# The last block of a fast-multiplication feed-forward kernel: another order of products, halves in the last product, other engines and queues for the outputs

## Chip, cores, metric

One core of one Trainium2 chip. The metric is the time of one execution on the device in microseconds (us), as the median of several executions. The profile's "span" is about 1.7 us shorter than this time (2424.1 beside 2425.77). "The kernel before" was timed again beside every other kernel on the same chip; the experiments ran on three chips, and its median there was 2425.88, 2425.92 and 2425.79.

## The reference

```python
# x: (8, 4096, 192) float32, weight: (8 heads, 7 taps)
w = softmax(weight, axis=-1)
y = causal_conv7(x, w)               # each head's 24 channels share 7 taps
y = y.reshape(32768, 192)
h = y @ w_in                         # (192, 2048)
g = h * (1.0 / (1.0 + np.exp(-h)))   # silu
out = g @ w_out                      # (2048, 192)
```

## The kernel before

The tokens are worked off in 32 blocks (`NB`) of 1024, each as two halves of 512 (`TB`). A block has an "up" phase (y @ w_in and silu) and a "down" phase (g @ w_out). Both replace eight products of quarter matrices by seven, at the price of sums and differences of operands and of results. In the down phase a block has four outputs, each 96 channels (`HD`) by 512 tokens: `c[0]` to `c[3]`. The products stand in six PSUM banks, `acc[0]` to `acc[5]`. The upper 96 rows of a bank hold one product, and its lower 32 rows a part of a product that is spread over three banks. Products with raw silu(h) need no work ahead of them; the others take differences `t(i)` that VectorE makes from `g`. "P1" is in `acc[0]`, "P3" in `acc[1]`; "C11" is `c[0]`.

The accumulators of the last weight group are finished in the order 0, 1, 2, 3, 5, 4; the last, bank 4, is one that uses differences:

```python
    def down(b, j):
        ...
        sets = ((1, 2, 0), (3, 2, 1), (6, 2, 2), (7, 4, 0), (5, 4, 1))
        every = slice(0, TB)
        for i in (0, 1, 2, 4, 3, 5) if j < NJ - 1 else (0, 1, 2, 3, 5, 4):
            if j == 0:
                accs[b][i] = bank()
            for e in range(2):
                if i < 5:
                    own, other, c = sets[i]
                    for q in range(NP):
                        lhs, rhs = forms[own]()
                        mm(i, q, every, lhs, q, rhs, e)
                    lhs, rhs = forms[other]()
                    mm(i, NP, every, lhs, c, rhs, e)
                # ... (i == 5: four matmuls of 128 columns)
                yield
```

The outputs are then sums of banks. A bank's rows are copied by ScalarE, and VectorE adds:

```python
    def merge(b, name):
        # ... ScalarE copies: x0..x2, y0..y2 (a bank's lower 32 rows), z1
        out_, u, v = {
            "M1": lambda: (c[1], c[0], acc[2][0:n, :]),
            "M2": lambda: (c[3], c[1], acc[1][0:n, :]),
            "M3": lambda: (c[2], c[1], acc[3][0:n, :]),
            "M4": lambda: (c[1], c[3], acc[4][0:n, :]),
            "M5": lambda: (c[3], c[2], acc[4][0:n, :]),
            "M6": lambda: (c[0], c[0], t["y"][0:n, :]),
            "M7": lambda: (c[2], c[2], t["x"][0:n, :]),
        }[name]()
        pin(nc.vector.tensor_tensor(out_, u, v, op=ALU.add))
```

VectorE transposes each output in tiles of 32 by 32, and it is stored in three pieces of 32 channels. Each piece is 64 KB. In the last block the pieces go over three queues:

```python
    def turn_out(b, i):
        ...
        pin(nc.vector.transpose(osb[...], cmbs[b][0][0:top, i, :]))
        for q in range(top // SQ):
            n, c = ...
            queue = (nc.sync, nc.scalar, nc.gpsimd)[q % 3] if b == NB - 1 else nc.sync
            queue.dma_start(
                out=out_v[2 * b + n][:, :, c : c + SQ], in_=osb[SQ * q : SQ * q + SQ, i, :, :]
            )
```

`pin` keeps an instruction at its place in its engine's program order.

Of the kernel before, what the change touches and what calls it, by code (L numbers as in the profile page):

```python
# [9 lines left out]
F32 = mybir.dt.float32  # L10
I32 = mybir.dt.int32
AF = mybir.ActivationFunctionType
ALU = mybir.AluOpType
# [4 lines left out]
def kernel(  # L18
# [24 lines left out]
    nc = tc.nc  # L43
# [6 lines left out]
    P = 128  # L50
# [4 lines left out]
    TB = 512  # L55
    TT = 2 * TB
    NB = NT // TT
    NCH = DFF // P
    NM = NCH // 2
    NJ = NM // 2  # L60
    SQ = 32
    HD = D // 2
    NP = HD // SQ
# [3 lines left out]
    out_v = out.rearrange("(n k t) d -> n t k d", k=TB // SQ, t=SQ)  # L67

    const = ctx.enter_context(tc.tile_pool(name="const", bufs=1))
    xpool = ctx.enter_context(tc.tile_pool(name="xp", bufs=1))  # L70
    tpool = ctx.enter_context(tc.tile_pool(name="tp", bufs=3))
    gpool = ctx.enter_context(tc.tile_pool(name="gp", bufs=2 * NJ))
    upool = ctx.enter_context(tc.tile_pool(name="up", bufs=13))
# [29 lines left out]
    def pin(ins):  # L103
        return tc.keep_in_program_order(ins)
# [8 lines left out]
    vec = Pinned(nc.vector)  # L113

    def bank():
        return psum.tile([P, TB], F32, tag="ps", name="ps")
# [3 lines left out]
    def load(b, ks=range(NK)):  # L120
# [14 lines left out]
        out=wexp.rearrange("p h k -> p (h k)"),  # L135
        in_=weight.rearrange("(o h) k -> o (h k)", o=1).to_broadcast([P, H * K]),
# [5 lines left out]
    for k in range(NK):  # L142
        nc.gpsimd.dma_start(
            out=xts[0][R:P, k, 0:pad], in_=x0[:, k, :], allow_slow_non_contiguous=True
# [142 lines left out]
    for e in range(2):  # L287
        half = hot[R * e : R * e + R]
        for sign, base in ((1, 0), (-1, grp - 1)):
            nc.gpsimd.affine_select(  # L290
                out=half,
                in_=half,
# [20 lines left out]
    for k in range(NK):  # L313
# [4 lines left out]
            op=ALU.mult,  # L318
# [96 lines left out]
    bk, us, sums, cmbs, accs = {}, {}, {}, {}, {}  # L415
# [63 lines left out]
        )[i]()  # L479
        pin(nc.vector.tensor_tensor(t[i // 2][:, i % 2, :], u, v, op=ALU.subtract))  # L480

    def down(b, j):



        if j == 0:
            accs[b] = {}
        g = [gs[b, j, a] for a in range(2)]
        w, x_ = wo[j], wx[j]

        def t(i):
            return sums[b, j][i // 2][:, i % 2, :].rearrange("p (e t) -> p e t", e=2)

        def mm(i, q, cols, lhs, c, rhs, e):
            pin(
                nc.tensor.matmul(  # L496
                    accs[b][i][SQ * q : SQ * q + SQ, cols],
                    lhs[:, e, SQ * c : SQ * c + SQ],
                    rhs[:, e, cols] if i < 5 else rhs[:, e, ts(q, TB // 4)],
                    start=j == 0 and e == 0,  # L500
                    stop=j == NJ - 1 and e == 1,
                    skip_group_check=True,
                )
            )

        a_ = [[w[:, a, :, HD * u : HD * u + HD] for a in range(2)] for u in range(2)]
        forms = {
            1: lambda: (a_[0][0], g[0][:, 0]),
            2: lambda: (a_[0][1], g[1][:, 0]),
            3: lambda: (x_[:, 2], g[1][:, 1]),  # L510
            4: lambda: (a_[1][1], t(3)),
            5: lambda: (x_[:, 0], t(0)),
            6: lambda: (x_[:, 1], t(1)),
            7: lambda: (a_[1][0], t(2)),
        }
        sets = ((1, 2, 0), (3, 2, 1), (6, 2, 2), (7, 4, 0), (5, 4, 1))
        every = slice(0, TB)

        for i in (0, 1, 2, 4, 3, 5) if j < NJ - 1 else (0, 1, 2, 3, 5, 4):
            if j == 0:  # L520
                accs[b][i] = bank()
            for e in range(2):
                if i < 5:
                    own, other, c = sets[i]
                    for q in range(NP):
                        lhs, rhs = forms[own]()
                        mm(i, q, every, lhs, q, rhs, e)
                    lhs, rhs = forms[other]()
                    mm(i, NP, every, lhs, c, rhs, e)
                else:  # L530
                    lhs, rhs = forms[4]()
                    for q in range(4):
                        mm(5, q, slice(0, TB // 4), lhs, 2, rhs, e)
                yield
        for a in range(2):
            del gs[b, j, a]
# [63 lines left out]
    osbs = {}  # L600

    def turn_out(b, i):
        if b not in osbs:
            osbs[b] = tpool.tile([P, 4, TB // SQ, SQ], F32, tag="t", name="osb")
        osb = osbs[b]
        top = HD if b else P
        pin(
            nc.vector.transpose(  # L608
                osb[0:top, i, :, :].rearrange("p k c -> p (k c)"), cmbs[b][0][0:top, i, :]
            )  # L610
        )
        for q in range(top // SQ):
            n, c = (i % 2, HD * (i // 2) + SQ * q) if b else (q // 2, R * i + SQ * (q % 2))
            queue = (nc.sync, nc.scalar, nc.gpsimd)[q % 3] if b == NB - 1 else nc.sync
            queue.dma_start(  # L615
                out=out_v[2 * b + n][:, :, c : c + SQ], in_=osb[SQ * q : SQ * q + SQ, i, :, :]
            )

    plan = [slot.split() for slot in PLAN.split("|")]
    NU = NM * 11 // 2  # L620
    did = set()

    def step(b, token):

        if token[0] == "-":
            b, token = b - 1, token[1:]
        name, arg = token.split(".") if "." in token else ("", "")
        if b < 0 or b >= NB or not name or (b, token) in did:
            return
        did.add((b, token))  # L630
        digits = [int(c) for c in arg]
        if name[0] in "PE":
            product(b, digits[0], name)
        elif name[0] in "sCg":
            if b:
                sums_h(b, name, digits[0])
        elif name == "t":
            sum_g(b, *digits)
        elif name[0] in "Mzyx":
            merge(b, name)  # L640
        elif name == "o":
            turn_out(b, *digits)
        elif b + 1 < NB:
            {"i": turn_in, "v": conv, "w": win}[name](b + 1, *digits)
            if name == "v" and digits[1] == K - 1 and (b, "down") in did:
                spread(b + 1, digits[0])
                if digits[0] == NK - 1 and b + 2 < NB:
                    load(b + 2)

    def begin_down(b):  # L650
        did.add((b, "down"))
        for k in range(NK):
            if b + 1 < NB and (b, f"v.{k}{K - 1}") in did:
                spread(b + 1, k)

    def run(b, slots):
        for s in slots:
            for token in s:
                step(b, token)


    for k in range(NK):
# [31 lines left out]
    for k in range(NK):  # L694
        turn_out(0, k)
# [3 lines left out]
    for b in range(1, NB):  # L699
        run(b, plan[: NU // 4])  # L700
        if b == 1:
            for j in range(NJ):
                combine_out(j)
        run(b, plan[NU // 4 : NU])
        begin_down(b)
        slots = (None for j in range(NJ) for _ in down(b, j))
        for s in plan[NU:]:
            next(slots)
            run(b, [s])
        assert next(slots, 0) == 0  # L710
    run(NB, plan[:NU])


# [28 lines left out]
```

## Time and profile before

All times below are on the trace's own clock, from the start of the span. The prediction shows the profile lines they come from. TensorE works without a break to 2412.22, so the first 99.5% of the span are not in question here; the tail behind it is.

| kernel before | us |
|---|---|
| median time | 2425.77 |
| span | 2424.1 |
| TensorE's end | 2412.22 |
| VectorE's last transpose ends | 2417.24 |
| last store issued (start): GpSimd's; SyncE and ScalarE 2417.27 | 2417.64 |
| last store landed | 2422.24 |
| end | 2424.07 |

The tail is read as a relay: TensorE's end, the last data in its final form, the last store's issue, its landing, the end.

### The profile page before, as it was taken

How to read it: one execution, taken by the hardware profiler on the slowest of the kernel's cores; microseconds unless marked ns; L12 is line 12 of the kernel's file. 1: busy time of each engine (PE TensorE's matmuls, PEld its weight loads, DVE VectorE, ACT ScalarE, POOL GpSimd, SP SyncE). 2: the span in 40 equal slices, each digit the busy share in tenths (PEclk: the TensorE clock that was granted, in tenths of full speed). 3: DMA queues.
4: the chain of work that ended last, by engine and by line, in shares of the span. 5: the costliest groups of instructions: out<-in, count | busy, mean ns of one | idle time of the engine just before them, and what ended most of it. 6: DMA issues, size and time to landing. Idle time of an engine off the chain costs nothing.

```text
span 2424.1 us, 43022 instructions
## 1 busy us (share of the span) xinstructions
PE 2389.0 (99%) x17744; PEld 944.2 (39%) x17744; DVE 2076.5 (86%) x2827; ACT 981.7 (40%) x1845; POOL 66.4 (3%) x100
## 2 busy tenths in 40 slices
PE   6999999999999999999999999999999999999998
PEld 3344433334433334333444333443334443334432
DVE  8988888898888888888988889888889888898875
ACT  3134533345433345333454333553334543335432
POOL 3300000000000000000000000000000000000000
PEclk9999999999999999999999999999999999999999
DMA  7321222222222212221222222122222222221220
GB/s 151 73 52 32 44 44 53 41 43 40 36 53 50 43 32 42 47 53 40 41 41 39 53 48 46 31 39 50 53 40 40 38 43 53 46 43 36 36 40 14
DMA packets 452005, 111.65 MB, mean 46 GB/s; under 512 B 421792, under 2 KB 426912, under 8 KB 451808
## 3 DMA queue, kind: packets, MB, share of 16 engines
q1 hardware_dynamic: 447888, 106.63, 23.6%
q8 instruction: 139, 2.28, 0.4%
q0 software_dynamic: 608, 1.84, 0.4%
q10 hardware_dynamic: 3312, 0.42, 0.1%
q14 instruction: 58, 0.48, 0.1%
HBM read 31.49 MB, written 25.17 MB: 23 GB/s over the span
## 4 chain that ended last, share of the span: by engine, by line
PE 98%; DVE 1%; DMA 0%; SPq 0%; ACT 0%; issue 0%; POOL 0%; ACTq 0%; POOLq 0%; DVEq 0%
PE ps L439 49%; PE ps L496 46%; PE ps L547 2%; PE ps L403 1%; DVE nat L353 0%; DVE two L111 0%; SPq L127 0%; DMA nat<-in_x_dram 0%; DVE cmb L598 0%; DMA raw<-in_moe_w_in_dram 0%; DVE mh L111 0%; DVE wr L111 0%; DVE xt L333 0%; POOL out_dram L615 0%; DVE osb L608 0%
## 5 line engine op out<-in xcount | busy, mean ns | idle before, releaser
L439 PE MATMUL ps<-dup,ws 64*128 64x512 f32 x2480 | 869.1, 589 | 0.0
L496 PE MATMUL ps<-g,wo 128*32 128x512 f32 x2976 | 662.0, 593 | 0.0
L463 DVE TENSOR_TENSOR g<-u,ps 128x512 f32<-128x512 f32 x744 | 485.6, 680 | 117.6 <-PE ps L439 88.8
L439 PE MATMUL ps<-win,wr 64*128 64x512 f32 x1488 | 568.8, 589 | 0.1
L496 PE MATMUL ps<-t,wo 128*32 128x512 f32 (+1 forms) x4464 | 500.7, 450 | 0.0
L460 ACT ACTIVATE g<-g 128x512 f32<-128x512 f32 x744 | 444.7, 631 | 99.9 <-DVE g L463 99.9
L439 PEld LDWEIGHTS ps<-dup,ws 64*128 64x128 f32 x2480 | 363.8, 187 | 289.5 <-issue 273.8
L496 PE MATMUL ps<-t,wx 128*32 128x512 f32 x2976 | 453.0, 592 | 0.0
L353 DVE SCALAR_TENSOR_TENSOR nat<-xt,taps,nat 128x512 f32<-128x512 f32 x576 | 432.0, 750 | 15.1
L439 PE MATMUL ps<-dup,wr 64*128 64x512 f32 x992 | 419.3, 596 | 0.0
L454 ACT COPY u<-ps 128x512 f32<-128x512 f32 x496 | 277.5, 588 | 228.7 <-PE ps L439 225.8
L586 ACT COPY cmb<-ps 96x512 f32<-96x512 f32 x31 | 18.0, 581 | 832.2 <-PE ps L496 832.2
L480 DVE TENSOR_TENSOR t<-g 128x1024 f32<-128x1024 f32 x248 | 299.8, 1220 | 26.7 <-PE ps L496 26.7
L480 DVE TENSOR_TENSOR t<-g,t 128x1024 f32<-128x1024 f32 x248 | 303.4, 1224 | 18.3 <-PE ps L496 7.4
L439 PEld LDWEIGHTS ps<-win,wr 64*128 64x128 f32 x1488 | 234.0, 187 | 174.6 <-issue 145.7
L496 PEld LDWEIGHTS ps<-t,wo 128*32 128x32 f32 x4464 | 178.3, 110 | 222.6 <-issue 205.2
L439 PE MATMUL ps<-win,ws 64*128 64x512 f32 x496 | 241.5, 589 | 0.0
L496 PE MATMUL ps<-g,wx 128*32 128x512 f32 x1488 | 234.7, 592 | 0.0
L496 PEld LDWEIGHTS ps<-t,wx 128*32 128x32 f32 x2976 | 121.9, 110 | 278.2 <-issue 268.7
L598 DVE TENSOR_TENSOR cmb<-cmb,ps 96x512 f32<-96x512 f32 x155 | 105.7, 682 | 141.9 <-ACT u L583 139.7
L439 PEld LDWEIGHTS ps<-dup,wr 64*128 64x128 f32 x992 | 160.8, 187 | 127.2 <-issue 112.0
L496 PEld LDWEIGHTS ps<-g,wo 128*32 128x32 f32 x2976 | 168.5, 110 | 97.7 <-issue 97.7
(56 smaller groups left out, 1194.6 us busy)
## 6 DMA issues: line engine op xcount, KB each, us to landing
dup<-nat SPq DMA_DIRECT2D x384, 128.0 KB, 2.3
nat<-in_x_dram SPq DMA_DIRECT2D x382, 64.0 KB, 2.4
out_dram<-osb SPq DMA_DIRECT2D x376, 64.0 KB, 2.0
raw<-in_moe_w_in_dram SPq DMA_DIRECT2D x16, 192.0 KB, 4.8
raw<-in_moe_w_out_dram SPq DMA_DIRECT2D x8, 384.0 KB, 3.6
ws<-wr POOLq DMA_DIRECT2D x8, 192.0 KB, 4.4
xt<-xt SPq DMA_DIRECT2D x31, 4.5 KB, 1.9
tail<-xt SPq DMA_DIRECT2D x24, 4.5 KB, 1.9
```

The source lines that it names most:

```text
L353: nc.vector.scalar_tensor_tensor(out=dst, in0=src, scalar=tap, in1=dst, op0=ALU.mult, op1=ALU.add)
L403: nc.tensor.matmul(hs[a, n, e], rows(wr[j], e)[:, a, k, :], rows(d, e)[:, n, k, :], start=k == 0, stop=k == NK - 1,)
L439: nc.tensor.matmul(bk[b, m, bn], rows(w, half), rows(v, half), start=first, stop=True, skip_group_check=True,)
L454: pin(copy(u, bk[b, m, "1"]))
L460: pin(nc.scalar.activation(g, g, AF.Silu))
L463: pin(nc.vector.tensor_tensor(g, us.pop((b, m, i)), bk[b, m, bn], op=ALU.add))
L480: pin(nc.vector.tensor_tensor(t[i // 2][:, i % 2, :], u, v, op=ALU.subtract))
L496: nc.tensor.matmul(accs[b][i][SQ * q : SQ * q + SQ, cols], lhs[:, e, SQ * c : SQ * c + SQ], rhs[:, e, cols] if i < 5 else rhs[:, e, ts(q, ...
L547: nc.tensor.matmul(acc[k][R * n : R * n + R, :], wo[j][:, a, e, R * k : R * k + R], gs[b, j, a][:, n, e, :], start=j == 0 and a == 0 and e ...
L586: pin(nc.scalar.copy(c[0], acc[0][0:n, :]))
L598: pin(nc.vector.tensor_tensor(out_, u, v, op=ALU.add))
```

## The change

The intent: let the products that need no differences come last in the last block; let four outputs be nearly complete by then, so that the last sums are short; let two outputs leave while TensorE still works; split the last product's columns into halves so that the first half is worked on while the second is computed. GpSimd takes the sum of C11. The stores use two queues (SyncE, ScalarE, SyncE) and no longer GpSimd's.

```diff
-    def down(b, j):
+    def out_slot(b, j, i, e, half=None):
+        ...   # the four matmuls of accumulator i, optionally for one half of the columns
...
-            queue = (nc.sync, nc.scalar, nc.gpsimd)[q % 3] if b == NB - 1 else nc.sync
-            queue.dma_start(
+            nc.sync.dma_start(
...
+    def finish(b):
+        late = (NJ - 2, NJ - 1)
+        for j in late:
+            ...                                   # differences
+            for i in (2, 4, 3, 5):
+                for e in range(2):
+                    out_slot(b, j, i, e)
+        ...
+        def store(i, cols, rows_=slice(0, n)):
+            ...
+            vec.transpose(osb[rows_, cols], cmb[rows_, i, cols])
+            for q in range(rows_.start // SQ, rows_.stop // SQ):
+                (nc.sync, nc.scalar, nc.sync)[q % 3].dma_start(...)
+        ...                                       # sums over accumulators 2 to 5
+        for j in late:
+            for e in range(2):
+                out_slot(b, j, 0, e)
+        for half in range(2):
+            for j in late:
+                for e in range(2):
+                    out_slot(b, j, 1, e, half)
+            if half == 0:
+                for k in (3, 2):
+                    add(c[k], c[k], acc[0][0:n, :])
+                    store(k, every)
+                add(c[1], c[1], acc[0][0:n, :])
+                pin(nc.scalar.copy(c[0], acc[0][0:n, :]))
+                pin(nc.scalar.copy(part(y, 0), acc[0][n:P, :]))
+        for half in range(2):
+            cols = slice(half * TB // 2, (half + 1) * TB // 2)
+            add(c[1][:, cols], c[1][:, cols], acc[1][0:n, cols])
+            pin(nc.scalar.copy(part(y, 1)[:, cols], acc[1][n:P, cols]))
+            store(1, cols)
+            nc.gpsimd.tensor_tensor(c[0][:, cols], c[0][:, cols], y[0:n, cols], op=ALU.add)
+            store(0, cols)
...
-    run(NB, plan[:NU])
+    finish(NB - 1)
```

More of the change, by code (lines that the diff above doesn't have):

```diff
@@ L480, in sum_g, with t @@
         pin(nc.vector.tensor_tensor(t[i // 2][:, i % 2, :], u, v, op=ALU.subtract))
-    def down(b, j):
-        if j == 0:
-            accs[b] = {}
+    def out_slot(b, j, i, e, half=None):
         g = [gs[b, j, a] for a in range(2)]
         w, x_ = wo[j], wx[j]
-        def t(i):
-            return sums[b, j][i // 2][:, i % 2, :].rearrange("p (e t) -> p e t", e=2)
-        def mm(i, q, cols, lhs, c, rhs, e):
-            pin(
-                nc.tensor.matmul(
-                    accs[b][i][SQ * q : SQ * q + SQ, cols],
-                    lhs[:, e, SQ * c : SQ * c + SQ],
-                    rhs[:, e, cols] if i < 5 else rhs[:, e, ts(q, TB // 4)],
-                    start=j == 0 and e == 0,
-                    stop=j == NJ - 1 and e == 1,
-                    skip_group_check=True,
-                )
-            )
+        if i not in accs.setdefault(b, {}):
+            accs[b][i] = bank()
+        def t(k):
+            return sums[b, j][k // 2][:, k % 2, :].rearrange("p (e t) -> p e t", e=2)
         a_ = [[w[:, a, :, HD * u : HD * u + HD] for a in range(2)] for u in range(2)]
@@ L515, in down @@
         }
-        sets = ((1, 2, 0), (3, 2, 1), (6, 2, 2), (7, 4, 0), (5, 4, 1))
-        every = slice(0, TB)
+        own, other, c = ((1, 2, 0), (3, 2, 1), (6, 2, 2), (7, 4, 0), (5, 4, 1), (4, 4, 2))[i]
+        for q in range(4):
+            lhs, rhs = forms[own if q < NP else other]()
+            k = c if i == 5 or q == NP else q
+            to = slice(0, TB // 4) if i == 5 else slice(0, TB) if half is None else ts(half, TB // 2)
+            pin(
+                nc.tensor.matmul(
+                    accs[b][i][SQ * q : SQ * q + SQ, to],
+                    lhs[:, e, SQ * k : SQ * k + SQ],
+                    rhs[:, e, ts(q, TB // 4) if i == 5 else to],
+                    start=j == 0 and e == 0,
+                    stop=j == NJ - 1 and e == 1,
+                    skip_group_check=True,
+                )
+            )
+    def down(b, j):
         for i in (0, 1, 2, 4, 3, 5) if j < NJ - 1 else (0, 1, 2, 3, 5, 4):
-            if j == 0:
-                accs[b][i] = bank()
             for e in range(2):
-                if i < 5:
-                    own, other, c = sets[i]
-                    for q in range(NP):
-                        lhs, rhs = forms[own]()
-                        mm(i, q, every, lhs, q, rhs, e)
-                    lhs, rhs = forms[other]()
-                    mm(i, NP, every, lhs, c, rhs, e)
-                else:
-                    lhs, rhs = forms[4]()
-                    for q in range(4):
-                        mm(5, q, slice(0, TB // 4), lhs, 2, rhs, e)
+                out_slot(b, j, i, e)
                 yield
@@ L659, in run, with part, add @@
                 step(b, token)
+    def finish(b):
+        late = (NJ - 2, NJ - 1)
+        for j in late:
+            for k in (0, 1, 3, 2):
+                step(b, f"t.{j}{k}")
+            for i in (2, 4, 3, 5):
+                for e in range(2):
+                    out_slot(b, j, i, e)
+        acc, n = accs[b], HD
+        cmb = xpool.tile([P, 4, TB], F32, tag="cmb", name="cmb")
+        cmbs[b] = [cmb]
+        c = [cmb[0:n, i, :] for i in range(4)]
+        y, x_ = (upool.tile([P, TB], F32, tag="u", name="u") for _ in range(2))
+        def part(t, k):
+            return t[SQ * k : SQ * k + SQ, :]
+        def add(out_, u, v):
+            vec.tensor_tensor(out_, u, v, op=ALU.add)
+        def store(i, cols, rows_=slice(0, n)):
+            if b not in osbs:
+                osbs[b] = tpool.tile([P, 4, TB // SQ, SQ], F32, tag="t", name="osb")
+            osb = osbs[b][:, i, :, :].rearrange("p k c -> p (k c)")
+            vec.transpose(osb[rows_, cols], cmb[rows_, i, cols])
+            ks = slice(cols.start // SQ, cols.stop // SQ)
+            for q in range(rows_.start // SQ, rows_.stop // SQ):
+                ch = HD * (i // 2) + SQ * q
+                (nc.sync, nc.scalar, nc.sync)[q % 3].dma_start(
+                    out=out_v[2 * b + i % 2][:, ks, ch : ch + SQ],
+                    in_=osbs[b][SQ * q : SQ * q + SQ, i, ks, :],
+                )
+        every = slice(0, TB)
+        pin(nc.scalar.copy(c[1], acc[2][0:n, :]))
+        pin(nc.scalar.copy(part(y, 2), acc[2][n:P, :]))
+        pin(nc.scalar.copy(part(x_, 1), acc[4][n:P, :]))
+        add(c[2], c[1], acc[3][0:n, :])
+        pin(nc.scalar.copy(part(x_, 0), acc[3][n:P, :]))
+        add(c[3], c[2], acc[4][0:n, :])
+        add(c[1], c[1], acc[4][0:n, :])
+        for q in range(4):
+            pin(
+                nc.scalar.copy(
+                    part(x_, 2)[:, ts(q, TB // 4)], acc[5][SQ * q : SQ * q + SQ, 0 : TB // 4]
+                )
+            )
+        add(c[2], c[2], x_[0:n, :])
+        for j in late:
[19 more added lines that the diff above has]
+            store(0, cols)
@@ L705 @@
         begin_down(b)
-        slots = (None for j in range(NJ) for _ in down(b, j))
-        for s in plan[NU:]:
-            next(slots)
+        last = b == NB - 1
+        if last:
+            did.update((b, t.lstrip("-")) for s in plan for t in s if t.lstrip("-")[0] in "Mzyxo")
+        slots = (None for j in range(NJ // 2 if last else NJ) for _ in down(b, j))
+        for s, _ in zip(plan[NU:], slots):
             run(b, [s])
         assert next(slots, 0) == 0
-    run(NB, plan[:NU])
+    finish(NB - 1)
 _INS = ['x', 'weight', 'moe_w_in', 'moe_w_out']
```

## The prediction

> **What bounds the kernel now.** I read the page first: the span, TensorE's busy share and the chain of work that ended last.
>
> ```profile
> span 2424.1 us, 43022 instructions
> PE 2389.0 (99%) x17744; PEld 944.2 (39%) x17744; DVE 2076.5 (86%) x2827; ACT 981.7 (40%) x1845; POOL 66.4 (3%) x100
> PE 98%; DVE 1%; DMA 0%; SPq 0%; ACT 0%; issue 0%; POOL 0%; ACTq 0%; POOLq 0%; DVEq 0%
> ```
>
> TensorE carries 98% of the chain. The change touches only the second half of the last of 32 blocks and keeps TensorE's column count, so it can win only where TensorE no longer works. The busy time by stretch says how much that is (columns: PE, weight loads, DVE, ACT, POOL; then clock, DMA share, GB/s):
>
> ```profile
> 2403.00:2412.30 9.30, 9.22 (x104) 2.92 (x96) 3.65 (x6) 3.92 (x9) 0.00 (x0) 1.00 0.01 2
> 2412.30:2424.10 11.80, 0.00 (x0) 0.00 (x0) 3.86 (x6) 0.58 (x1) 2.61 (x4) 0.64 0.40 67
> ```
>
> TensorE ends at 2412.22; the remaining 11.85 us (0.5% of the span) are the tail, and all that is at stake. The chain in order of time shows its first half:
>
> ```profile
> 2412.28 0.38 ACTq L615
> ...
> 2412.70 0.59 ACT u L583
> ...
> 2413.31 0.70 DVE cmb L598
> ...
> 2414.03 0.69 DVE cmb L598
> ...
> 2414.75 0.69 DVE cmb L598
> 2415.43 0.63 DVE osb L608
> 2416.07 0.28 issue
> 2416.35 1.29 POOL out_dram L615 x2
> 2417.64 0.64 POOLq L737
> ```
>
> ScalarE first issues a store (0.38), then copies the last bank's lower rows (0.59); VectorE makes three dependent sums (about 0.72 each) and three transposes (0.6 apart), so the last stores start at 2417.27. Then only stores and the closing remain. SyncE's waits and the landing times of the stores issued after 2417.2 show the second half:
>
> ```profile
> SPq L737 <- DMA out_dram<-osb: 4.5, 1, 4.5
> ```
> ```profile
> out_dram<-osb POOLq DMA_DIRECT2D x2, 64.0 KB, 4.3
> out_dram<-osb SPq DMA_DIRECT2D x1, 64.0 KB, 4.6
> out_dram<-osb ACTq DMA_DIRECT2D x1, 64.0 KB, 4.8
> ```
>
> They take 4.3 to 4.8 us, because nine of the twelve stores of 64 KB are issued within 1.6 us (2416.08 to 2417.64). The three issued near 2412.3 had the engines to themselves:
>
> ```profile
> out_dram<-osb SPq DMA_DIRECT2D x1, 64.0 KB, 2.1
> out_dram<-osb ACTq DMA_DIRECT2D x1, 64.0 KB, 2.4
> out_dram<-osb POOLq DMA_DIRECT2D x1, 64.0 KB, 2.7
> ```
>
> The last landing is at 2422.25, the end at 2424.07: closing takes 1.8 us. The tail is thus 5.05 (sums to last issue) + 5.0 (backlog of stores) + 1.8.
>
> **What the Trainium skill says.** (1) "PSUM — Partial Sum Buffer", section "PSUM bank collisions raise a hardware error": two engines must not touch one bank and 32-partition quadrant at once, even in different columns; guard by bank. The built program agrees: in the changed kernel VectorE's first half-sum from P3's bank waits for TensorE's count 8888, the last matmul of the second half. No run yet shows it in time. (2) "DMA: Bandwidth & Descriptors", "Issuing engines are not separate DMA queues": stores from several queues share the same DMA engines, and only issue time is saved. The trace agrees: three queues, and still 4.3 to 4.8 us under backlog against 2.1 to 2.7. (3) "GPSIMD Engine Reference", "Elementwise — side-by-side cycle accounting": about 2.6 cycles an element for a two-input float32 add (at its 1.2 GHz 2.2 ns). The trace has it on an idle chip, at 584 ns for 192 elements and 456 for 128, so 2.0 ns an element:
>
> ```profile
> L254 POOL TENSOR_TENSOR wo<-wo 128x192 f32<-128x192 f32 x4 | 2.2, 584 | 0.0
> L254 POOL TENSOR_TENSOR wr<-wr 128x128 f32<-128x128 f32 x3 | 1.3, 456 | 0.1
> ```
>
> **The change, part by part.** *TensorE.* The last two weight groups first give accumulators 2, 4, 3 and 5, which use differences, then accumulator 0, then accumulator 1 (P3) in two halves of 256 columns. A quad of 512-column matmuls takes 0.43 us, one of 128 columns 0.107, so it is linear and 256 columns cost 0.215. The order of sums on VectorE (due 2392 to 2400) stays ahead of their use. From 2393.99: differences done at 2405.1, accumulator 0 at 2408.6, first half of P3 at 2410.3, all at 2412.0 plus 0.2 of drain. TensorE's end stays at 2412.2: gain 0.
>
> *Hidden under TensorE.* The four sums over accumulators 2 to 5 run from 2405.0 to 2408.1. Accumulator 0 is readable at 2408.8; then VectorE does sum, transpose, sum, transpose, sum (pitches of 0.6 to 0.72), to 2412.17. So six of the twelve stores are issued at 2410.3 to 2412.0 and land by about 2414.5. Before, only three were out by then. Backlog mostly gone.
>
> *On the path after TensorE.* Durations of halves are estimates from the rows: VectorE 0.684 us for 512 columns less 256/0.96 ns = 0.42; transpose 0.40; ScalarE 0.579 and 0.255 for 512 and 128 give 0.36; GpSimd 0.456 + 128 x 2.0 ns = 0.71, plus 0.08 to start.
> - VectorE's half sum 2412.31 to 2412.74. But since VectorE reads accumulator 0 first, ScalarE's two copies of that bank (0.58 each) start only after VectorE's third sum, at 2412.22, and end at 2413.39; P3's half copy follows, to 2413.77.
> - GpSimd half 0: 2413.85 to 2414.56. VectorE's transpose of it to 2415.0, and only then, in program order, the second half sum, 2414.95 to 2415.37.
> - ScalarE has meanwhile two stores ahead of its second copy; it copies 2415.45 to 2415.81; GpSimd half 1 2415.9 to 2416.6; last transpose to 2417.05.
>
> So the last data is ready at 2417.05, just 0.2 us earlier than before: two serial half chains (2.7 and 2.1 us) take the place of one chain of full size.
>
> *Stores.* The three after that are 32 KB each. SyncE carries two of each three. Every store waits for the previous one on its semaphore of eight: SyncE's second-half store of c1 waits for a ScalarE store issued at 2415.04 (lands near 2417.0), the first of the last pair for one issued at 2415.83 (lands near 2417.8). I take 2417.85 and 2418.2 for the last two issues, 0.35 later than data alone would allow for each. A half-size store without backlog: 2.1 less some 0.3 = 1.8 us, landing at 2420.0. The saving against 2422.25 is 2.25 us.
>
> *Closing.* Before, the first of nine waits in a row was the last store's (a GpSimd one), and the eight others followed at 0.06 each. Now the last to land is among the final three: 0.4 less, so 1.4. End 2421.4 against 2424.07: 2.65 less. I give 0.1 back for unmodelled queue steps: 2425.77 - 2.57 = 2423.2.
>
> **The rivals.** *Halves overlap as intended*: if the first half's sum started when its matmuls end (2410.5), the first half chain would hide and the end fall 2 us more, to about 2421.2. For it speaks the code's order; against it the wait for count 8888. *GpSimd slow*: beside VectorE's work the trace shows 0.77 us for 128 elements instead of 0.456; if that held at 256, each half costs about 0.5 more, and two of them 1 us: 2424.2. Against it: VectorE waits at that moment. *Stores still bound*: if landings stay near 3 to 4 us or the semaphore chain on SyncE slips by one landing more, 2424.3 to 2425. *TensorE stalls* on differences or on 256-column weight loads (0.13 us per quad of loads, under 0.215 of matmul): 0.3 to 1 us back; the stretches show no idle time, so unlikely.
>
> **Range and chances.** The gain can hardly pass the tail less one bare chain (sum, copy, add, transpose, store, closing: about 6.5 us). Each term above is uncertain by some 0.3, GpSimd and the store waits by 0.5 to 1, mostly on the slow side: 2422.3 to 2424.3. 2% is 48.5 us, four times the whole tail, so within 2% is nearly certain: faster 0.003, within 0.995, slower 0.002.
>
> **What would show each step.** TensorE's end within 0.2 us of 2412.2, without idle time. No VectorE sum from P3's bank before it. ScalarE's two copies of accumulator 0 right after VectorE's third sum of it, ahead of P3's first half copy. GpSimd adds near 0.7 us each, 2 us apart. Last store issued near 2418.2, landing within 2 us; waits of SyncE for landed stores between its own. A half sum starting near 2410.5, GpSimd adds over 1 us, or last landings of 3 us and more would show the prediction wrong, as would a tail shorter than 8 us or longer than 10.5.

## The result, and the profile after

The kernel after took 2423.11 us in the median of six runs (2422.77 to 2423.26), beside 2425.83 for the kernel before in six (2425.73 to 2426.24): 2.72 us less. The ratio is 0.9988 (interval 0.9975 to 1.0001). Ratios here and below are the mean time of one kernel's fast runs over the mean of the other's fast runs of the same rounds, so not quite the ratio of the quoted medians. The interval reaches 1, but the two sets of runs lie 2.5 us apart at their nearest, and each set is only 0.5 us wide; I take the 2.7 us as real for that reason. The traced run is the fastest of the six: its span is 2421.0, those of the others 2421.2 to 2421.5.

First the page of the kernel after, with span and busy times:

```profile
span 2421.0 us, 43109 instructions
PE 2389.7 (99%) x17776; PEld 953.3 (39%) x17776; DVE 2077.5 (86%) x2831; ACT 983.3 (41%) x1847; POOL 65.3 (3%) x98
```

TensorE's busy time has not fallen; it has 32 more, shorter matmuls. Then the busy time by stretch of the kernel after (same columns as in the prediction):

```profile
2403.00:2412.30 9.30, 9.16 (x132) 3.89 (x124) 5.96 (x10) 2.30 (x7) 0.00 (x0) 1.00 0.11 17
2412.30:2421.00 8.70, 0.00 (x0) 0.00 (x0) 2.42 (x6) 1.78 (x4) 1.44 (x2) 0.75 0.49 75
```

TensorE's last matmul still ends at 2412.2, and the stretch behind it has shrunk from 11.8 to 8.7 us. VectorE now works 5.96 us of the last stretch under TensorE, against 3.65 before, and the DMA share there is 0.11 against 0.01: that is what was moved forward. The chain of the kernel after, in order of time, is the leg from accumulator 0 to the last data:

```profile
2411.52 0.58 DVE cmb L111
...
2412.18 0.53 ACT cmb L714
...
2412.77 0.58 ACT u L715
...
2413.53 0.23 ACT u L719
...
2413.82 0.72 POOL cmb L721
2414.54 1.33 issue
2415.87 0.77 POOLq L802
...
2416.66 0.44 DVE osb L111
```

VectorE's third sum from P1's bank ends at 2412.10; only then ScalarE copies that bank (in two copies), then P3's first half, and GpSimd adds. The row "issue 1.33" hides a second round through all engines: VectorE transposes the first half's result, makes the second half's sum (2414.95), ScalarE copies (2415.47), GpSimd adds again (2415.91 to 2416.63). The last data is final at 2417.10, as late as before.

SyncE's waits on landed stores at the store line (L682), and the landing times of the stores issued from 2417 on:

```profile
SPq L682 <- DMA out_dram<-osb: 1.5, 3, 0.7
```
```profile
out_dram<-osb SPq DMA_DIRECT2D x3, 32.0 KB, 1.6
out_dram<-osb ACTq DMA_DIRECT2D x1, 32.0 KB, 1.6
```

SyncE waits three times, 0.7 us at most, for an earlier store to land before it can issue the next. The last of these waits ends at 2417.40, when a ScalarE store has landed; the next-to-last store is issued at 2417.48, the last one at 2418.15, a microsecond after the data. But a store, now of half the size, lands in 1.6 us (median; the last one took 1.86), where the kernel before needed 4.3 to 4.8.

| leg, us | before | predicted | after |
|---|---|---|---|
| TensorE's end | 2412.22 | 2412.2 | 2412.16 |
| last data final | 2417.24 | 2417.05 | 2417.10 |
| last issue | 2417.64 | 2418.2 | 2418.15 |
| last landing | 2422.24 | 2420.0 | 2420.00 |
| end | 2424.07 | 2421.4 | 2421.04 |

By legs: the last issue is 0.51 later, the landing after it 2.75 shorter (4.61 to 1.86), the closing 0.79 shorter (1.83 to 1.04). Sum: 3.03 less in the traces, and 2.7 in the medians.

So the reorganised arithmetic gave almost nothing on the data's own leg (0.1); the time came out of the stores and the closing. Which part of the change did that is the question of the experiments.

### The profile page after: what moved, and what is told of

It is laid out like the page before. It is cut to its first block, busy times and chain, and to the rows that moved or that the text cites. A ratio compares the mean times of both kernels' runs of the same rounds, so it can differ in the third digit from the quotient of the medians.

```text
span 2421.0 us, 43109 instructions
## 1 busy us (share of the span) xinstructions
PE 2389.7 (99%) x17776; PEld 953.3 (39%) x17776; DVE 2077.5 (86%) x2831; ACT 983.3 (41%) x1847; POOL 65.3 (3%) x98
## 4 chain that ended last, share of the span: by engine, by line
PE 98%; DVE 1%; DMA 0%; SPq 0%; issue 0%; ACT 0%; POOLq 0%; POOL 0%; ACTq 0%; DVEq 0%
PE ps L439 49%; PE ps L510 46%; PE ps L538 2%; PE ps L403 2%; DVE nat L353 0%; SPq L127 0%; DMA nat<-in_x_dram 0%; DMA raw<-in_moe_w_in_dram 0%; DVE two L111 0%; DVE cmb L111 0%; DVE osb L111 0%; DVE xt L333 0%; DVE nat L350 0%; ACT two L201 0%; DVE mh L111 0%
## 5 line engine op out<-in xcount | busy, mean ns | idle before, releaser
L510 PE MATMUL ps<-g,wx 128*32 128x512 f32 (+1 forms) x1512 | 234.6, 585 | 0.0
```

The source lines that it names most:

```text
L510: nc.tensor.matmul(accs[b][i][SQ * q : SQ * q + SQ, to], lhs[:, e, SQ * k : SQ * k + SQ], rhs[:, e, ts(q, TB // 4) if i == 5 else to], sta ...
```

## The experiments

Theory A (the prediction's): the halves on TensorE do nothing, because VectorE may read P3's bank only after its last matmul; the serial half chains cost what they save; the gain is that six stores leave early. The rivals are named with each run. Twelve kernels ran, all with correct results.

The traces start up unevenly. In the kernel after and in experiment 3, which are the same program up to the last sums, the same matmul starts at 170.95 and at 171.28 us, and TensorE ends at 2412.16 and 2412.49; over all kernels its end lies between 2412.06 and 2412.50. Where a leg is compared between two traces below, it is therefore counted from TensorE's end. In the kernel after the last data is final 4.94 us behind it, the last store issued at 5.98, landed at 7.84, and the end comes at 8.88; in the kernel before the four are 5.03, 5.42, 10.03 and 11.86.

**1. P3 in one piece on TensorE** (halves stay in the sums and stores).

```diff
-        for half in range(2):
+        for half in range(1):
             for j in late:
                 for e in range(2):
-                    out_slot(b, j, 1, e, half)
+                    out_slot(b, j, 1, e)
```

> P3 in one piece of 512 columns on TensorE; the sums, copies and stores after it still by halves. Theory A (the gain is the stores of two outputs that leave under TensorE; TensorE's halves do nothing, as the first half sum waits for the last matmul anyway): the first half sum starts at the same 2412.2, the time stays within 0.2 us of the changed kernel's 2423.1. Rival B (halves overlap TensorE with the sums): the half sum starts later and the time rises by 1 us or more.

Measured: 2422.90 (2422.63 to 2423.54), ratio 0.9988. The first half sum started at 2412.13 against 2412.23, 0.07 us behind TensorE's end in both. Halves on TensorE are worth nothing here, as Theory A has it.

**2. No halves at all**: experiment 1, and sums, copies and stores of whole outputs.

```diff
-        for half in range(2):
-            cols = ...
-            add(c[1][:, cols], ...); copy(part(y, 1)[:, cols], ...); store(1, cols)
-            nc.gpsimd.tensor_tensor(c[0][:, cols], c[0][:, cols], y[0:n, cols], op=ALU.add)
-            store(0, cols)
+        add(c[1], c[1], acc[1][0:n, :])
+        pin(nc.scalar.copy(part(y, 1), acc[1][n:P, :]))
+        store(1, every)
+        nc.gpsimd.tensor_tensor(c[0], c[0], y[0:n, :], op=ALU.add)
+        store(0, every)
```

> No halves anywhere: P3 whole, one sum of 512 columns, one copy, one GpSimd add, whole stores. Theory A: one chain takes the place of two serial half chains: sum to 2412.95, ScalarE's P1 copies to 2413.36, copy to 2413.95, GpSimd 1.23 us to 2415.25, transpose to 2415.95, last store near 2416.35, landing after 2.3, closing 1.05: end near 2419.8, so 1.2 us below the changed kernel (about 2421.9). Rival B: slower than the changed kernel by 0.5 us or more, because nothing is pipelined any more.

Measured: 2421.81 (2421.62 to 2422.13), ratio 0.9983. GpSimd's timeline in this kernel (start, duration, engine and form; in brackets the idle time ahead and what ended it) and the last row of its chain, VectorE's last transpose, show why:

```profile
2414.06 1.26 POOL L719 TENSOR_TENSOR cmb<-cmb,u 96x512 f32<-96x512 f32 x1 [168.81 <-ACT u L717]
```
```profile
2415.35 0.71 DVE osb L111
```

One GpSimd sum of 1.26 us replaces two of 0.72 with a whole round between them, so the last data is final at 2416.06 instead of 2417.10, and there are 12 stores instead of 18 (8 instead of 12 on SyncE), the last issued at 2416.45. The halves of sums and stores thus *cost* 1.1 us, against experiment 1, which differs in nothing else (1.3 against the kernel after): the split was made for an overlap that doesn't occur.

**3. P1's three sums first**, then ScalarE's copies of that bank, then the transposes.

```diff
-                for k in (3, 2):
-                    add(c[k], c[k], acc[0][0:n, :])
-                    store(k, every)
-                add(c[1], c[1], acc[0][0:n, :])
+                for k in (3, 2, 1):
+                    add(c[k], c[k], acc[0][0:n, :])
                 pin(nc.scalar.copy(c[0], acc[0][0:n, :]))
                 pin(nc.scalar.copy(part(y, 0), acc[0][n:P, :]))
+                for k in (3, 2):
+                    store(k, every)
```

> Halves kept; VectorE makes its three sums from P1's bank one after the other, then the transposes, so that ScalarE can copy P1's bank from 2410.7 on instead of 2412.2. Theory A: P3's first half copy then starts at 2412.7 instead of 2413.4, everything after it 0.7 us earlier: about 2422.4. Rival (ScalarE's copies are not on the path; the end hangs on stores alone): within 0.2 us of 2423.1, or slower, as the two hidden outputs leave later.

Measured: 2422.99 (2422.90 to 2423.07), a miss. Counted from TensorE's end, the last data was final 0.75 us earlier (4.19 instead of 4.94), as expected, but SyncE issued its last store at 5.93 instead of 5.98, and it landed at 7.81 instead of 7.84. SyncE waited four times for a landed store, 1.0 us in all (three times and 1.5 in the kernel after). With these 18 stores, data that comes earlier meets a queue that isn't free: the rival, that the end hangs on the stores, is right here.

**4. VectorE sums C11** in place of GpSimd.

```diff
-            nc.gpsimd.tensor_tensor(c[0][:, cols], c[0][:, cols], y[0:n, cols], op=ALU.add)
+            add(c[0][:, cols], c[0][:, cols], y[0:n, cols])
```

> C11 summed on VectorE instead of GpSimd, the rest as changed. Theory A: 0.42 us in place of 0.72 plus 0.08 to start, twice on the path: 0.7 us earlier, about 2422.4. Rival C (GpSimd relieves a busy VectorE): slower by 0.3 us or more, because VectorE has three more kinds of work there.

Measured: 2422.66 (2422.58 to 2422.98). The half sum took 0.42 us on VectorE against 0.72 on GpSimd and the last data was final 0.7 earlier (2416.39), but the last issue was only 0.4 earlier (2417.73), and the last landing 0.15 (2419.85), as that store took 2.12 us instead of 1.86. GpSimd costs 0.7 on the data's leg; the stores pass on less of it, 0.45 by the medians and 0.14 by the two traces.

**5. Sums first, halves only up to the transpose, whole stores.** Experiment 3, with the stores of outputs 1 and 0 sent whole after the second half.

```diff
             store(1, cols)              # now: transpose only
+            if half:
+                send(1, every)
             nc.gpsimd.tensor_tensor(c[0][:, cols], c[0][:, cols], y[0:n, cols], op=ALU.add)
             store(0, cols)              # now: transpose only
+        send(0, every)
```

> As the run with VectorE's three sums first (halves kept in sums, copies and transposes), but all four outputs leave in whole stores, 12 instead of 18. After that run the theory is: in the changed kernel the end hangs on SyncE's queue of stores, whose last three wait for landings of earlier ones, so earlier data gained 0.1 us only. Then with whole stores the earlier data counts: last data near 2416.4, last issue 2416.8, landing 2419.1, closing 1.05: time near 2421.9, 1.1 below. Rival (it is the number of bytes in flight, or the sums themselves): no better than 2422.7.

Measured: 2422.22 (2422.08 to 2422.54). Against experiment 3 the stores alone changed, and it is 0.77 faster: counted from TensorE's end, the last issue came at 4.61 instead of 5.93, although a whole store has to wait for both halves; the landing (2.75 instead of 1.88) gave 0.9 of that 1.3 back. It is 0.3 slower than I expected.

**6. Whole pieces, sums first, VectorE for C11**: the three findings together (2, 3 and 4).

```diff
+                for k in (3, 2, 1):
+                    add(c[k], c[k], acc[0][0:n, :])
                 ...   # ScalarE's copies of acc[0]
+                for k in (3, 2):
+                    store(k, every)
+        add(c[1], c[1], acc[1][0:n, :])
+        pin(nc.scalar.copy(part(y, 1), acc[1][n:P, :]))
+        store(1, every)
+        add(c[0], c[0], y[0:n, :])
+        store(0, every)
```

> No halves, VectorE's three sums of P1's bank first, C11 summed on VectorE. If the terms of the path add up: P3's sum to 2412.95, copy to 2413.53, VectorE's sum of C11 to 2414.25, transpose to 2415.0, last issue 2415.45, landing 2.4, closing 1.1: end 2419.0, time near 2420.7, 1.1 below the run without halves. If ScalarE's copies or GpSimd were not on the path: 2421.5 or more.

Measured: 2421.05 (2421.02 to 2421.31), ratio 0.998 (0.9965 to 0.9995). The last data was final at 2415.26, 2.82 us behind TensorE's end instead of 4.94; the last issue came at 2415.94, but the landing after it takes 2.8 us again. Against experiment 2 that is 0.8 less, where I expected 1.1.

**7. P3's halves in two banks**, and GpSimd for C11 by halves, whole stores. This tests the bank wait itself: if the wait for TensorE's last matmul comes from the shared bank, another bank must remove it.

```diff
+        if i == 1 and half is None and b == NB - 1:
+            for h in range(2):
+                out_slot(b, j, i, e, h)
+            return
+        key = 6 if half == 1 else i
...
-                    accs[b][i][SQ * q : SQ * q + SQ, to],
+                    accs[b][key][SQ * q : SQ * q + SQ, to],
...
+        p3 = (acc[1], acc[6])
+        def sum_p3(half):
+            ...   # half of c[1] and of c[0] from bank p3[half]
                 for k in (3, 2, 1):
                     add(c[k], c[k], acc[0][0:n, :])
                 ...   # ScalarE's copies of acc[0]
+                store(3, every)
+                sum_p3(0)
+                store(2, every)
+        sum_p3(1)
+        store(1, every)
+        store(0, every)
```

> P3's halves in two PSUM banks of their own, three sums first, C11 on GpSimd by halves, whole stores. If the wait for the last matmul came from the one bank that both halves share, VectorE's first half sum now starts at about 2411.2, before TensorE's end, ScalarE's half copy at about 2412.0, and only the second half's chain is left after the end: GpSimd to 2413.85, transpose to 2414.55, last issue 2415.0, landing 2.4, closing 1.05: end 2418.5, time near 2420.2. If the half sum still starts at 2412.2, the bank is not the reason.

Measured: 2421.10 (2420.93 to 2421.16). VectorE's timeline in this kernel:

```profile
2411.39 0.38 DVE L111 TENSOR_TENSOR cmb<-cmb,ps 96x256 f32<-96x256 f32 x1
...
2414.06 0.71 DVE L111 STREAM_TRANSPOSE osb<-cmb 96x512 f32<-96x512 f32 x1 [0.49 <-POOL cmb L716]
```

The first half sum runs at 2411.39, ahead of TensorE's end (2412.3 in this run). The fair partner is experiment 5, with the same order of VectorE's sums and one bank; VectorE's line there:

```profile
2412.17 0.42 DVE L111 TENSOR_TENSOR cmb<-cmb,ps 96x256 f32<-96x256 f32 x1 [0.36 <-PE ps L510]
```

VectorE is free from 2411.81 on and waits 0.36 us, until TensorE has ended (2412.10). So it is the shared bank that makes the program wait, and the halves overlap once they have banks of their own. In the kernel after, though, the bank cost only 0.14 us: there VectorE was busy with its sums and transposes until 2412.09, so that two banks alone, without the new order (which no run tried), could hardly have started the first half sum earlier. The last data is final 2.42 us behind TensorE's end, 2.5 earlier than in the kernel after. Yet the time is no better than experiment 6, 0.9 above what I expected. Busy time by stretch of this kernel shows where it went (the last three columns are clock, DMA share, GB/s):

```profile
2415.00:2416.00 1.00, 0.00 (x0) 0.00 (x0) 0.00 (x0) 0.00 (x0) 0.00 (x0) 1.00 1.10 169
2416.00:2417.00 1.00, 0.00 (x0) 0.00 (x0) 0.00 (x0) 0.00 (x0) 0.00 (x0) 0.95 0.84 113
2417.00:2418.00 1.00, 0.00 (x0) 0.00 (x0) 0.00 (x0) 0.00 (x0) 0.00 (x0) 0.50 1.06 157
```

No engine computes, and the DMA engines are busy at a share of 0.84 to 1.10. SyncE's last four store issues stretch to 0.58 to 0.79 us, the last is at 2415.99, and it lands at 2418.53. The sums are no longer what the end waits for.

**8. Early stores held back, first attempt.** The stores of outputs 3 and 2 were moved behind the last GpSimd sum in the source, to see what leaving early is worth.

```diff
+            if i > 1:
+                held.append(i)      # sent after GpSimd's second half sum
```

> The changed kernel, but the six stores of the two outputs that are ready before TensorE's end are held back and issued just before the last three half stores; the rest of the work is the same. Theory A (their early leaving is what the change gains): the backlog is back, the last landings take 3 us and more again, and the time rises by 1.4 to 2.5 us, to 2424.5 to 2425.6, close to the kernel before. Rival (the gain is from the sums and the closing, stores overlap anyway): within 0.4 us of 2423.1.

Measured: 2423.17 (2423.01 to 2423.37), as the kernel after. This is no test: the trace shows five of the six stores at their old place (2410.46 to 2411.78) and only the sixth late, at 2417.14. They weren't pinned to their place in the program, and by the record's account the layer that orders the instructions left them where they were. The run stands as little more than a repeat of the kernel after.

**9. The same, with those stores pinned.**

```diff
+                if pinned or i > 1:
+                    pin(move)       # move: the store
```

> The experiment with held stores again; the first try did not hold them, because unpinned stores are put in their engines' order by the recording layer, which left them where they were. Now the six stores of the two early outputs are pinned behind ScalarE's last half copy, so they leave from 2415.9 on. Theory A (their early leaving is what the change gains): the backlog is back, last landing near 2421.5 to 2422.5, time 2424.5 to 2425.6, near the kernel before. Rival (the gain is from the sums and the closing): within 0.4 us of 2423.1.

Measured: 2424.59 (2424.44 to 2424.67), ratio 0.9995. The data is final 4.94 us behind TensorE's end, exactly as in the kernel after, but the last store is issued at 7.63 instead of 5.98 and lands at 9.35 instead of 7.84. The early departure of two outputs is worth 1.5 us of the 2.7, against holding them until 2416.4 to 2418.9 as here.

**10. The kernel after with GpSimd's queue as third.**

```diff
-                (nc.sync, nc.scalar, nc.sync)[q % 3].dma_start(
+                (nc.sync, nc.scalar, nc.gpsimd)[q % 3].dma_start(
```

> The changed kernel with the third store of each output on GpSimd's queue again, as before. Each such issue takes GpSimd 0.65 us, some ahead of its two adds, and its store was the slowest to land. Theory: the second add starts 0.6 to 0.9 us later, last landing 1 us later, and the closing waits are again headed by a GpSimd store: time 2423.9 to 2424.8. Rival (SyncE's queue is the bound, a third queue relieves it): 2422.9 or less.

Measured: 2424.73 (2424.64 to 2424.91), ratio 0.9996: 1.6 us worse than the kernel after. Its chain, in order of time:

```profile
2415.74 0.56 POOL out_dram L682
...
2416.50 0.58 POOL out_dram L682
...
2417.09 0.73 POOL cmb L721
```

GpSimd issues stores, 0.58 us each, ahead of its second sum, which so starts at 2417.09 instead of 2415.91 (1.0 later counted from TensorE's end). A GpSimd store was also the last to land, at 2421.42, and the closing took 1.5.

**11. The kernel before with two queues**: the reverse of 10, so the change of queues and nothing else.

```diff
-            queue = (nc.sync, nc.scalar, nc.gpsimd)[q % 3] if b == NB - 1 else nc.sync
+            queue = (nc.sync, nc.scalar, nc.sync)[q % 3] if b == NB - 1 else nc.sync
```

> The kernel before with only its stores changed: two queues instead of three in the last block. Theory: the same backlog of nine stores (landing near 2422), but the closing is 0.6 to 0.8 shorter because no GpSimd store heads the nine waits: time 2424.9 to 2425.3. Rival (two queues cost issue time that three would save): 2425.9 or more.

Measured: 2424.29 (2424.07 to 2424.39), ratio 0.9994: 1.5 us better than the kernel before, where I expected 0.5 to 0.9. VectorE's last transpose ends 5.03 us behind TensorE's end, as in the kernel before. The last issue is 1.9 us *later* (7.33 instead of 5.42, SyncE now carries two thirds), but the last landing is 0.6 earlier (9.43 instead of 10.03) and the closing 0.9 instead of 1.83: six tenths of the gain lie in the closing. Busy time by stretch, the kernel before first, then this one:

```profile
2418.00:2419.00 1.00, 0.00 (x0) 0.00 (x0) 0.00 (x0) 0.00 (x0) 0.28 (x1) 0.50 0.84 125
2419.00:2420.00 1.00, 0.00 (x0) 0.00 (x0) 0.00 (x0) 0.00 (x0) 0.00 (x0) 0.50 0.71 119
2420.00:2421.00 1.00, 0.00 (x0) 0.00 (x0) 0.00 (x0) 0.00 (x0) 0.00 (x0) 0.50 0.80 132
```
```profile
2418.00:2419.00 1.00, 0.00 (x0) 0.00 (x0) 0.00 (x0) 0.00 (x0) 0.00 (x0) 0.50 1.04 150
2419.00:2420.00 1.00, 0.00 (x0) 0.00 (x0) 0.00 (x0) 0.00 (x0) 0.00 (x0) 0.50 0.82 120
2420.00:2421.00 1.00, 0.00 (x0) 0.00 (x0) 0.00 (x0) 0.00 (x0) 0.00 (x0) 0.50 1.07 160
```

With GpSimd's queue the same backlog moves at 119 to 132 GB/s in these three microseconds, without it at 120 to 160. The share of the DMA engines doesn't say the same of both queues: in the kernel before, from 2412 to 2425, GpSimd's 0.26 MB go as 128 packets of 2 KB and take 7.7% of the engines' time, SyncE's and ScalarE's 0.26 MB each as 2112 packets of some 124 bytes and take 14.1 and 14.4%. Why the backlog with GpSimd's stores lands later all the same, no run here shows.

**12. Experiment 6 with output 3 stored right after its own sum**, to fill the DMA engines earlier, since 6 and 7 looked bound by them.

```diff
                 for k in (3, 2, 1):
                     add(c[k], c[k], acc[0][0:n, :])
+                    if k == 3:
+                        store(3, every)
```

> The best so far without halves (sums first, C11 on VectorE), but the third output is transposed and stored right after its own sum, and the other two sums follow. In the two best runs the DMA engines were full from 2413 to 2418: 12 stores at about 0.55 us each set the end. Here the first stores leave 1.1 us earlier (2410.2). Theory: last data again near 2415.0, last landing near 2417.9 instead of 2418.7, time 2420.3 to 2420.6. Rival (the last data and SyncE's issues set the end, not the DMA engines): 2421.0 as in the other run, or more.

Measured: 2421.05 (2420.81 to 2421.24), ratio 0.998 (0.9967 to 0.9994), a miss by half a microsecond: equal to experiment 6. The first stores left earlier and the DMA share was 0.63 to 0.86 in the four microseconds from 2412 on, so no longer full; but the last data was final at 2415.33, as in 6, and from there issue (0.4), landing (2.6) and closing (1.2) followed. So "the DMA engines are full" doesn't explain the floor at 2421.05 alone, and neither do the sums, which were 0.4 us earlier in 7, counted from TensorE's end, for the same time.

## Why the prediction was right

**TensorE: gain 0.** Right: its end moved by 0.06, less than it moves between traces of one program. Experiment 1 shows that its halves are without effect, experiments 5 and 7 that a shared bank makes VectorE wait. The prediction named the bank alone; that VectorE itself is busy until 2412.09 stands in its own timetable (2412.17), and either alone would have kept the first half sum until about TensorE's end.

**Hidden under TensorE: six stores leave early.** Right in place: their issues ran from 2410.23 to 2412.41, predicted 2410.3 to 2412.0. Experiment 9 prices it at 1.5 us.

**The path after TensorE.** Right in mechanism and size: two serial half chains with the last data at 2417.10, predicted 2417.05. GpSimd's halves took 0.718 and 0.720, predicted 0.71. VectorE's half sum took 0.416, predicted 0.42. The Trainium skill comes close to it: "VectorE: DVE Perf Modes", section "The TRN2 errata — SBUF-src ops pay a fixed extra latency per instruction", has (N+151)/0.96 ns for a float32 add, so by estimate 424 ns at 256 columns and 691 at 512, where the traces show 416 to 421 and about 684 for an add that follows a wait (and 378 for the second half sum, which starts before the transpose ahead of it has ended). What the prediction took as unchangeable, the split, costs 1.1 us (experiment 2 against 1).

**Stores.** The mechanism held: SyncE waits for landings, and the last store lands 1.86 us after its issue (1.8). That the last issue agrees (2418.15, predicted 2418.2) is in part luck: the store before it, expected at 2417.85 behind a landing at 2417.8, went at 2417.48 behind a landing at 2417.40, and a pause of 0.34 us that no landing explains made up for it. The prediction's reading of the kernel before was also 0.37 early here: its last issue is 2417.64, so the tail's sum is 5.4 + 4.6 + 1.8, not 5.05 + 5.0 + 1.8. What the prediction missed is *why* the backlog went. It gave all of it to the six early stores. Experiment 11 shows that leaving GpSimd's queue is worth 1.5 us even without any early store, experiment 10 that going back to it costs 1.6. Queue and early stores, 1.5 each, add to more than 2.7, because the rest of the change costs something: from the kernel before the medians go 1.5 down with the queues alone (experiment 11), 0.3 up with the new arithmetic while its early stores are held (9), and 1.5 down when these leave early (the kernel after).

**Closing: the mis-sized term.** Predicted 0.4 shorter, measured 0.79. What the prediction blamed, the place of the last store's wait in SyncE's row of nine, is right and has the size that it gave: after the last landing the row takes another 0.55 us in the kernel before (all nine waits) and 0.17 in the kernel after (three). It left out a second cost of the same size. In the kernel before SyncE's row is through at 2422.79, but the common end of all engines starts only at 2423.31, where it starts 0.1 us after the row in the kernel after and in experiment 11. In between lie the end of GpSimd's longest drain (an instruction of the program's closing) at 2422.91, 0.67 us after its last store has landed, and SyncE's own drain, not before 2423.14. GpSimd's drains at the closing line (ns, shortest, median and longest; first and last start):

```profile
L737 POOLq DRAIN  x3: 40/102/5397, 2417.5 to 2423.8; - x3
```

In experiment 10, where a GpSimd store is the last to land again, this drain ends 0.75 us after that landing and the closing takes 1.5, though SyncE's row is short there (0.08). Where GpSimd has no late store, the common end takes 0.75 to 0.77 us and the whole closing 0.9 to 1.2, for the most part by the place in the row. The drain is the one record that fits the gap; no experiment changed it alone.

That this error does not show in the total is luck. The tail behind TensorE's end was predicted as 9.2 us and measured as 8.88; the traced run is the fastest of six, and TensorE's end alone moves by 0.3 us and more between traces.

**The rivals.** "Halves overlap as intended" fell (experiment 1) and came true with two banks (7), though its predicted 2 us weren't paid out. "GpSimd slow" fell: 0.72, not 1.2. "TensorE stalls" fell: no idle time in the last stretches. "Stores still bound" was the nearest: not for the kernel after against the prediction, but for every attempt to go beyond it (3, 6, 7).

**A better version.** Experiments 6, 7 and 12 take 2421.05 to 2421.10, 2.1 us below the kernel after and 4.7 to 4.9 below the kernel before (ratio 0.998): a fifth of a per cent.

**What stays open.** SyncE's last store in the kernel after and in experiments 1, 3, 4 and 8 comes some 0.34 us later than data, landings and its own queue explain (2418.15 in the kernel after, where 2417.80 would have been possible). The floor of experiments 6, 7 and 12 is not attributed: busy DMA engines in 7, the last store's own issue, landing and closing in 12. And why the stores run at 150 to 169 GB/s at best, over a microsecond: "DMA: Bandwidth & Descriptors", section "Specifications", asks for pieces of 512 bytes or more, and nearly all packets of these stores are smaller (4752 of 4753 in experiment 11 from 2417 to 2424); no run here changed the pieces.

## What to carry to other kernels

Behind a saturated TensorE, follow the tail leg by leg to the end: data that is final earlier is worth only what the store issue, the landing and the closing pass on, and here data that was 2.5 us earlier paid no more than data that was 2.1 us earlier. Split a last product by columns only if each half has its own bank and the engine that reads it is free by then, and don't split the stores with it; a split that cannot overlap costs the extra rounds. Try the choice of store queues by itself before rebuilding the arithmetic: one line gave more than half of the gain of the whole change, most of it in the closing.

## What the Trainium skill lacked or had wrong

- "DMA: Bandwidth & Descriptors", section "Issuing engines are not separate DMA queues", says that several issuing engines save only issue time. Here the choice of queue had a price of its own that this section doesn't have: without GpSimd's queue the kernel before was 1.5 us faster although its last issue came 1.9 us later, and with it the kernel after was 1.6 us slower. The slower first byte that the section "Specifications" gives for GpSimd's path (about 1 us against 0.6) points the same way, as do lone stores before (2.7 us against 2.1 and 2.4), but it is smaller than what was measured, of which 0.9 us lie in the closing.
- The same page: no figure for how long a store issue holds GpSimd itself, next to its arithmetic. A store issue held GpSimd for 0.58 us (32 KB) to 0.68 us (64 KB), and its second sum in experiment 10 came 1.0 us late.
- No page has the time from the last landing to the end of the profiled program in its parts: 0.9 to 1.2 us where SyncE or ScalarE issued the last stores, 1.5 to 1.8 where a GpSimd store was the last and GpSimd's drain ended 0.67 to 0.75 us after its landing.
- "PSUM — Partial Sum Buffer", section "PSUM bank collisions raise a hardware error", lacks nothing for the rule: disjoint columns of one bank collide too, and the program is guarded accordingly (a wait of 0.36 us with one bank in experiment 5, none with two in 7). What a page could add is the consequence, that an output split by columns within one bank can't be read early, half by half. No run here let two engines touch one bank at once.
